# Attention with a mixture of experts: the squares kept in memory as turned, stored in 2 KB runs and read in 512-byte runs

## The chip, the cores and the metric

The kernel runs on one core of a Trainium2 chip. The metric is the device time of one execution in microseconds. Of the version before there are three runs: 2153.48, 2156.42 and 2159.98 us, median 2156.42 us.

## The reference, cut to what matters

There are 8 batches of 2496 tokens with 256 channels. Attention has no softmax: its weights are squares of clipped scores, and the scores are of z with itself, so that the matrix of weights is symmetric. Then each row goes through the one expert of eight that its gate picks.

```python
scores = scale * np.matmul(z, z.transpose(0, 2, 1))     # symmetric; z is 8 x 2496 x 64
attn = np.maximum(scores, 0.0) ** 2
out = np.matmul(attn, v)                                # v is 8 x 2496 x 256
x = (u * out).reshape(B * S, D)
...
e_idx = np.argmax(logits, axis=1)                       # logits = x @ w_gate + bias of the modality
h = np.maximum(x[mask] @ w1[e], 0.0)
out[mask] = gate_w[mask, None] * (h @ w2[e])
```

## The kernel before, in words

**Two parts.** The first part is the attention with the gate and the scattering of rows to their experts; it ends at about 1279 us. The second part runs the experts over tiles of 512 rows and is not touched by the change.

**Chunks and steps.** In the attention part each batch has five chunks of query columns, four of width 512 and a last one of 448. A chunk is worked through in ten steps, one for each pair of key tiles (2 x 128 keys). A step holds a tile r of 128 partitions (keys) x 2 x 512 (the two key tiles, the chunk's queries). For a step that is computed afresh, TensorE (PE) makes the scores (`scores`, line 334), ScalarE (ACT) clips and scales them (`root`, line 345) and squares them (`square`, line 394). Every step then has its squares split into a rounded part ah (`high`, line 418, on ACT or VectorE) and a rest al (`low`, line 427, on VectorE, called DVE), and PE multiplies both with the values v into the accumulators (`weigh`, line 451). `low` stands on DVE always, so PE waits for DVE in every step.

**Turned squares.** Since the matrix is symmetric, the block of keys q and queries c is the transpose of the block of keys c and queries q. For most pairs of chunks the kernel computes one of the two, transposes it on DVE in blocks of 32 x 32 (`turn_squares`, line 364, into one of two buffers named turn), stores it in memory (`store_squares`, lines 377 and 381) and reads it back when the other chunk needs it (`load_turned`, line 354), in place of scores, root and square. Of diagonal blocks one half is treated so (`is_half`: one half of the columns is computed, the other is read). In memory a block is a 512 x 512 matrix in the order in which the reader wants it. So the blocks of 32 x 32, which the transpose leaves in their places among the partitions, have to be put in order by the store: one transfer for each group of 32 partitions, with runs of 64 floats (256 bytes), in the last step of a chunk six transfers with runs of 32 floats. The load is then one transfer with runs of 4 KB for each partition.

**Who sets the order.** A planner in the kernel lists all pieces of work with an estimated cost and the step by which they are due, plays five queues (PE, ACT, DVE, GpSimd, SyncE's DMA queue) with these costs, and emits the instructions of each engine in the order in which the pieces came up. The order is then fixed; each engine works through its own in order and waits where an input or a buffer is missing. The costs are constants in the source: a transpose stands with 1.18 us (0.62 for a half), a store and a load with the numbers that the change edits. Pieces marked "AD" (`high`) go to whichever of ACT and DVE is free in that play. Buffers: six tiles r (tag a), four ah, four al, two turn.

```python
x = st_a[g].rearrange("p n (t i) -> p n t i", i=BLK)                      # turn_squares
nc.vector.transpose(out=y.rearrange(order, n=2)[:, :, t], in_=x[:, :, t])
...
src = squares[i // 2, c, b % 2].rearrange("(s p k) q -> s p k q", s=2, k=2)  # load_turned
nc.sync.dma_start(out=a[:, :, :w], in_=src[i % 2, :, :, :w])
```

Other lines that the text speaks of: 565 sums the gate's partial products (`take_gates`, a reduction over elements 32 bytes apart), 589 and 647 are small reductions of the routing (over neighbours, and over elements 80 bytes apart), 888 is the transpose of the second part, 547 and 557 turn the rows of a finished chunk, 507 and 511 evacuate its accumulators.

Of the kernel before, what the change touches and what calls it, by code (L numbers as in the profile page):

```python
# [9 lines left out]
F32 = mybir.dt.float32  # L10
# [6 lines left out]
P = 128  # L17
T = 512
# [9 lines left out]
def tile_attention_moe(ctx: ExitStack, tc: tile.TileContext, ut, v, zt, mid, wg, mb, w1, w2, out):  # L28
# [41 lines left out]
    xs = dram.tile([E * CAP, XW], F32, name="xs")  # L70
    places = dram.tile([MAXT, 2], I32, name="places")
    pairs |= {(c, c) for c in range(NCH - 1)}
    squares = {(q, c, e): dram.tile([T, T], F32, name=f"squares{q}_{c}_{e}") for q, c in pairs for e in range(2)}


    ident_r = const.tile([P, P], F32R, name="ident")
# [228 lines left out]
    def is_half(g):  # L305
        b, c, i = steps[g]
        return halved(b, c) and i == 2 * c + 1
# [8 lines left out]
    def is_turned(g):  # L316
        b, c, i = steps[g]
        return i // 2 < c and turns(b, i // 2, c)
# [18 lines left out]
    def root(g):  # L337
        w = columns(g)
        s = st_s.pop(g)
        if is_half(g):  # L340
            r = st_a[g]
        else:
            r = bulk.tile([P, 2, T], F32, tag="a", bufs=NA, name="r") if g else first_root
        for t in range(2) if g < 2 else (slice(0, 2),):
            nc.scalar.activation(out=r[:, t, w], in_=s[t][:, w] if g < 2 else s[:, :, w], func=AF.Relu, scale=INV)  # L345
        st_s[g] = r

    def load_turned(g):

        b, c, i = steps[g]  # L350
        w = H if is_half(g) else width[c]
        a = bulk.tile([P, 2, T], F32, tag="a", bufs=NA, name="r")
        src = squares[i // 2, c, b % 2].rearrange("(s p k) q -> s p k q", s=2, k=2)
        nc.sync.dma_start(out=a[:, :, :w], in_=src[i % 2, :, :, :w])
        st_a[g] = a

    def turn_squares(g):

        b, c, i = steps[g]
        y = raw.tile([P, T // BLK, 2 * BLK], F32, tag="turn", bufs=2, name="turn")  # L360
        order = "p t (i n) -> p n t i" if i < NI - 1 else "p t (n i) -> p n t i"
        t = slice(H // BLK if i == 2 * c else 0, T // BLK)
        x = st_a[g].rearrange("p n (t i) -> p n t i", i=BLK)
        nc.vector.transpose(out=y.rearrange(order, n=2)[:, :, t], in_=x[:, :, t])  # L364
        st_t[g] = y

    def store_squares(g):

        b, c, i = steps[g]
        y = st_t.pop(g)  # L370
        dst = squares[c, i // 2, b % 2].rearrange("(t i) k -> i t k", i=BLK)
        for n in range(P // BLK):
            mine = y[n * BLK:(n + 1) * BLK]
            if i < NI - 1:
                k0 = i % 2 * H + n * 2 * BLK
                t = slice(H // BLK if i == 2 * c else 0, T // BLK)
                nc.sync.dma_start(out=dst[:, t, k0:k0 + 2 * BLK], in_=mine[:, t])  # L377
            else:
                for k in range(2 if n < 2 else 1):
                    k0 = (J // 2 + k) * P + n * BLK  # L380
                    nc.sync.dma_start(out=dst[:, :, k0:k0 + BLK], in_=mine[:, :, k * BLK:(k + 1) * BLK])  # L381

    roots = {}

    def square(g):
        w = columns(g)
        a = r = st_s.pop(g)
        if g < 2:

            a = bulk.tile([P, 2, T], F32, tag="a", bufs=NA, name="r")  # L390
            roots[g] = r
        for t in (range(2),) if g else ((0,), (1,)):
            t = slice(t[0], t[-1] + 1)
            nc.scalar.square(out=a[:, t, w], in_=r[:, t, w])  # L394
        st_a[g] = a

    def first_high(g):
# [14 lines left out]
    def high(g):  # L412
        if g in roots:
            return first_high(g)
        w = width[steps[g][1]]
        ah = bulk.tile([P, 2, T], F32R, tag="ah", bufs=DEPTH, name="ah")
        copy = {"D": nc.vector.tensor_copy, "A": nc.scalar.copy}[by[g]]
        copy(out=ah[:, :, :w], in_=st_a[g][:, :, :w])  # L418
        st_h[g] = ah

    def low(g):
        _, c, i = steps[g]
        w = width[c]
        a, ah = st_a[g], st_h[g]
        al = bulk.tile([P, 2, T], F32R, tag="al", bufs=DEPTH, name="al")
        if i < NI - 1:
            nc.vector.tensor_tensor(out=al[:, :, :w], in0=a[:, :, :w], in1=ah[:, :, :w].bitcast(F32), op=ALU.subtract)  # L427
        else:
            nc.vector.tensor_tensor(out=al[:, 0, :w], in0=a[:, 0, :w], in1=ah[:, 0, :w].bitcast(F32), op=ALU.subtract)
            nc.vector.tensor_tensor(  # L430
                out=al[64:P, 1, :w], in0=a[64:P, 1, :w], in1=ah[64:P, 1, :w].bitcast(F32), op=ALU.subtract
            )
        st_h[g] = (ah, al)
# [551 lines left out]
    def step_pieces(n):  # L985
        b, c, i = steps[n]
        f = scale[c]
        high_after = None
        hold_a = Hold("a", 1 + is_source(n))
        read = None  # L990
        if is_turned(n) or is_half(n):
            src = [stored[b, i // 2, 2 * c + k] for k in range(1 if is_half(n) else 2)]
            read = transfer(0.7 if is_half(n) else 1.4, n - LEAD - (4 if is_half(n) else 2.5), load_turned, n, after=src, take=[hold_a], gate=n - LEAD - (6.0 if is_half(n) else 4))
            high_after = (read, 0.2)
        if not is_turned(n) and n >= MADE:
            f /= 1 + is_half(n)
            hold_s = Hold("s")
            p = piece(
                "P", 0.69 * f, n - LEAD, scores, n, after=[done_z.get((b, c)), done_z.get((b, i // 2)), scored.get("last")],
                take=[hold_s], drop=[hold_z[k] for k in {(b, c), (b, i // 2)}],  # L1000
            )
            scored["last"] = (p, 0.0)
            p = piece("A", 0.95 * f + 0.06, n - LEAD + 0.3, root, n, after=[(p, 0.25), (read, 0.2)], take=() if read else [hold_a], drop=[hold_s])
            p = piece("A", 0.95 * f + 0.06, n - LEAD + 1.0, square, n, after=[p])
            f = scale[c]
            high_after = (p, 0.08)
        if n > 0:
            own = n in (1,)
            p = piece(
                "D" if own else "AD", 1.3 if own else 0.93 * f, n - 1.8, high, n,  # L1010
                after=[high_after, (read, 0.2), split.get("high")], take=[Hold("ah")],
                drop=[Hold("a")] if n == 1 else (),
            )
            split["high"] = (p, 0.0)
            hold_h = [p.take[0], Hold("al")]
            if is_source(n):
                hold_t = Hold("turn")
                t = piece("D", 0.62 if i == 2 * c else 1.18, n - 1.5 if i == 2 * c else n + 0.5, turn_squares, n, after=[high_after], take=[hold_t], drop=[hold_a])
                stored[b, c, i] = transfer(1.4 if i == 2 * c else 2.8, n - 1.4 if i == 2 * c else n + 0.4, store_squares, n, issues=4 if i < NI - 1 else 6, after=[t])
                later.append((stored[b, c, i], hold_t))  # L1020
                begun.append(stored[b, c, i])
            p = piece(
                "D", 1.16 * f + 0.05, n - 1.1, low, n, after=[(p, 0.12), split.get("low")], take=hold_h[1:], drop=[hold_a],
            )
            split["low"] = (p, 0.0)
            ready = [(split["high"][0], 0.15), (p, 0.15 - 1.75 * f)]
        else:
            hold_h, ready = [Hold("ah"), Hold("al")], []
        v_of = hold_v[b, i // 2]
        ready += [done_v.get((b, i // 2)), weighed.get("last")]  # L1030
        first = i == first_step[b, c]
        if first:
            own = acc_hold[b, c] = [[Hold("bank") for _ in range(2)] for _ in range(KD)]
        us = (2.74 if i < NI - 1 else 2.05) * f
        if first and n:
            p = begun_chunk["half"] = piece("P", us / 2, n, weigh, n, 0, after=ready, take=own[0])
            p = piece("P", us / 2, n + 0.1, weigh, n, 1, after=[(p, 0.0)], take=own[1], drop=hold_h + v_of)
        elif n > 1 and i == second_step[b, c] and i < NI - 1:
            ready[-1] = (begun_chunk["half"], 0.0)
            h = piece("P", us / 2, n - 0.95, weigh, n, 0, after=ready)  # L1040
            p = piece("P", us / 2, n, weigh, n, 1, after=[(h, 0.0), weighed["last"]], drop=hold_h + v_of)
        else:
            p = piece("P", us, n, weigh if n else issued, n, after=ready, take=own[0] + own[1] if first else (), drop=hold_h + v_of)
        weighed["last"], weighed[n] = (p, 0.0), p
        p.step = n
# [508 lines left out]
```

## Time and profile before

| what | value |
|---|---|
| runs, median (lowest to highest) | 2156.42 us (2153.48 to 2159.98) |
| profiled execution, its own time | 2161.44 us |
| its span in the profile | 2159.0 us |
| PE, DVE, ACT busy in the span | 2128.9, 1650.3, 1422.8 us |
| mean granted clock of TensorE | 0.995 |
| bytes moved | 373.21 MB in 605497 packets |
| packets under 512 bytes | 522810 |
| transposes of squares | 189 (158 full, 31 half) |
| loads of turned squares | 189 |

How to read the rows. A row of a group names line, engine, operation, output and inputs, shape and count; then the busy time in us and the mean of one in ns; then the engine's idle time before these instructions and what ended it. A row of a stretch gives its bounds and length, and for each engine its busy time with the number of instructions; where it is asked for one line, those instructions alone are counted. A row of waits reads: who waited for whom, total us, times, longest. A row of the chain that ended last gives start, length and what it is. DMA share is the mean busy share of the 16 DMA engines.

### The profile page before, as it was taken

How to read it: one execution, taken by the hardware profiler on the slowest of the kernel's cores; microseconds unless marked ns; L12 is line 12 of the kernel's file. 1: busy time of each engine (PE TensorE's matmuls, PEld its weight loads, DVE VectorE, ACT ScalarE, POOL GpSimd, SP SyncE). 2: the span in 40 equal slices, each digit the busy share in tenths (PEclk: the TensorE clock that was granted, in tenths of full speed). 3: DMA queues.
4: the chain of work that ended last, by engine and by line, in shares of the span. 5: the costliest groups of instructions: out<-in, count | busy, mean ns of one | idle time of the engine just before them, and what ended most of it. 6: DMA issues, size and time to landing. Idle time of an engine off the chain costs nothing.

```text
span 2159.0 us, 44814 instructions
## 1 busy us (share of the span) xinstructions
PE 2128.9 (99%) x17190; PEld 1900.2 (88%) x17190; DVE 1650.3 (76%) x2292; ACT 1422.8 (66%) x2031; POOL 351.5 (16%) x342
## 2 busy tenths in 40 slices
PE   9999999999999999999999999999999999999997
PEld 7889999989989988888999988888888888888886
DVE  8889888878889889888888876666666666666664
ACT  8668868869768769779778753455455555454553
POOL 0000220210220210210310503112121211112121
PEclk9999999999999999999999999999999999999999
DMA  8976977977877978968968843645454544545451
GB/s 180 260 229 140 236 215 145 233 204 147 222 213 145 232 208 168 240 188 176 251 167 177 240 123 98 179 121 163 127 161 133 145 149 132 161 126 166 120 156 36
DMA packets 605497, 373.21 MB, mean 173 GB/s; under 512 B 522810, under 2 KB 547642, under 8 KB 605274
## 3 DMA queue, kind: packets, MB, share of 16 engines
q1 hardware_dynamic: 590186, 329.06, 60.8%
q0 software_dynamic: 15088, 41.21, 5.1%
q8 instruction: 136, 2.23, 0.4%
q14 instruction: 87, 0.71, 0.1%
HBM read 237.84 MB, written 132.31 MB: 171 GB/s over the span
## 4 chain that ended last, share of the span: by engine, by line
PE 86%; DMA 4%; issue 3%; DVE 3%; ACT 2%; SPq 1%; POOL 0%; POOLq 0%; DVEq 0%; ACTq 0%
PE acc L451 41%; PE ph L1268 18%; PE po L1279 12%; PE s L334 6%; PE po L1283 6%; DMA out_dram<-y,ids 2%; PE po L547 2%; DMA squares<-turn 1%; DMA r<-squares 1%; DVE al L427 1%; SPq L377 1%; ACT r L345 1%; ACT r L394 1%; DVE turn L364 0%; SPq L381 0%
## 5 line engine op out<-in xcount | busy, mean ns | idle before, releaser
L451 PE MATMUL acc<-ah,vh 64*128 64x512 f32 (+1 forms) x3120 | 468.6, 386 | 3.5 <-DVE ah L418 3.3
L451 PE MATMUL acc<-al,vh 64*128 64x512 f32 (+1 forms) x3120 | 456.5, 383 | 3.9 <-DVE al L427 3.9
L451 PE MATMUL acc<-ah,vl 64*128 64x512 f32 (+1 forms) x3120 | 455.9, 383 | 0.0
L427 DVE TENSOR_TENSOR al<-r,ah 128x1024 fp32r<-128x1024 f32 (+1 forms) x359 | 421.4, 1184 | 37.5 <-ACT ah L418 32.4
L1268 PE MATMUL ph<-xh,w 128*128 128x512 f32 x1248 | 399.5, 390 | 0.1
L1273 DVE SCALAR_TENSOR_TENSOR hl<-ph,hh 128x512 fp32r<-128x512 f32 x312 | 211.4, 688 | 236.3 <-ACT hh L1272 209.9
L1272 ACT ACTIVATE hh<-ph 128x512 fp32r<-128x512 f32 x312 | 187.1, 600 | 303.3 <-PE ph L1268 236.1
L671 POOL DMA_INDIRECT xs<-x,sloti x160 | 193.8, 1211 | 1076.4 <-ACT ah L418 492.6
L451 PEld LDWEIGHTS acc<-al,vh 64*128 64x128 f32 x3120 | 342.0, 185 | 28.6 <-DVE al L427 5.1
L451 PEld LDWEIGHTS acc<-ah,vh 64*128 64x128 f32 x3120 | 337.2, 185 | 28.7 <-DVE ah L418 3.7
L451 PEld LDWEIGHTS acc<-ah,vl 64*128 64x128 f32 x3120 | 337.3, 185 | 23.6
L418 ACT CAST ah<-r 128x1024 fp32r<-128x1024 f32 (+1 forms) x281 | 285.7, 1033 | 78.9 <-PE acc L451 46.6
L1279 PE MATMUL po<-w,hh 128*128 128x512 f32 x1248 | 296.7, 389 | 0.0
L345 ACT ACTIVATE r<-s 128x1024 f32<-128x1024 f32 (+2 forms) x244 | 235.7, 967 | 83.8 <-PE s L334 72.4
L1268 PEld LDWEIGHTS ph<-xh,w 128*128 128x128 f32 x1248 | 234.6, 188 | 47.8 <-issue 0.6
L1279 PEld LDWEIGHTS po<-w,hh 128*128 128x128 f32 x1248 | 234.1, 188 | 48.3
L1292 POOL DMA_INDIRECT out_dram<-y,ids x157 | 152.7, 973 | 721.2 <-DVE y L1320 686.2
L364 DVE STREAM_TRANSPOSE turn<-r 128x1024 f32<-128x1024 f32 (+1 forms) x189 | 217.0, 1151 | 41.1 <-DMA squares<-turn 27.6
L394 ACT ACTIVATE r<-r 128x1024 f32<-128x1024 f32 (+2 forms) x243 | 242.8, 999 | 5.7
L1268 PE MATMUL ph<-xl,w 128*128 128x512 f32 x624 | 243.7, 391 | 0.1
L334 PE MATMUL s<-zm 64*128 64x512 f32 (+2 forms) x1452 | 211.9, 383 | 5.2 <-ACT r L345 4.9
L869 DVE TENSOR_TENSOR w<-wq,w 128x1024 fp32r<-128x1024 f32 x148 | 177.8, 1221 | 19.3 <-ACT w L865 19.0
(158 smaller groups left out, 2013.1 us busy)
## 6 DMA issues: line engine op xcount, KB each, us to landing
wq<-in_moe_w_dram SPq DMA_DIRECT2D x148, 512.0 KB
squares<-turn SPq DMA_DIRECT2D x508, 128.0 KB
r<-squares SPq DMA_DIRECT2D x96, 512.0 KB
r<-squares SPq DMA_DIRECT2D x62, 448.0 KB
ut<-in_ut_dram SPq DMA_DIRECT2D x40, 512.0 KB
xg<-xs SPq DMA_DIRECT2D x156, 128.0 KB
squares<-turn SPq DMA_DIRECT2D x310, 64.0 KB
vr<-in_v_dram SPq DMA_DIRECT2D x32, 512.0 KB
```

What stands on the lines that cost most here:

```text
L334: nc.tensor.matmul(out=s[t][:, w], lhsT=lhs, rhs=mv[halves[t], ql, w], start=n == 0, stop=n == 2)
L345: nc.scalar.activation(out=r[:, t, w], in_=s[t][:, w] if g < 2 else s[:, :, w], func=AF.Relu, scale=INV)
L364: nc.vector.transpose(out=y.rearrange(order, n=2)[:, :, t], in_=x[:, :, t])
L394: nc.scalar.square(out=a[:, t, w], in_=r[:, t, w])
L418: copy(out=ah[:, :, :w], in_=st_a[g][:, :, :w])
L427: nc.vector.tensor_tensor(out=al[:, :, :w], in0=a[:, :, :w], in1=ah[:, :, :w].bitcast(F32), op=ALU.subtract)
L451: nc.tensor.matmul(out=acc[b, c][r][dh][:, :w], lhsT=V[b, k // J][y][halves[r], k % J, dh * P:(dh + 1) * P], rhs=x[halves[r], k % 2, :w], ...
L671: nc.gpsimd.indirect_dma_start(out=xs, out_offset=bass.IndirectOffsetOnAxis(ap=RT[b]["sloti"][:n, k:k + 1], axis=0), in_=x[:n, j, :], in_o ...
L1268: nc.tensor.matmul(out=ph, lhsT=lhs, rhs=rhs[:, k, :], start=n == 0, stop=n == 3 * KD - 1)
L1272: nc.scalar.activation(out=hh, in_=ph, func=AF.Relu)
L1273: nc.vector.scalar_tensor_tensor(out=hl, in0=ph, scalar=0.0, in1=hh.bitcast(F32), op0=ALU.max, op1=ALU.subtract)
L1279: nc.tensor.matmul(out=po[j], lhsT=x, rhs=both, start=f == 0, stop=False, skip_group_check=True)
```

## The change

Squares now lie in memory as the transpose leaves them, by partition and not by key. The tile in memory is [half of the chunk's columns, key tile of the pair, 128 partitions, 512]. The store is one transfer for each block, 2 KB runs on the memory side. The load puts the groups of 32 partitions in order: for each partition eight runs of 128 floats (512 bytes). For that the columns that go into one 32 x 32 block are no longer 32 neighbours but every eighth of 256 columns, so that 8 such blocks of a half lie behind each other in a stored row.

What a load brings is then, within a partition, in groups of 64 columns that alternate between the two key tiles (`blocks`); `high` and `low` read it in that order through `views` and write their parts ah and al in the old order. In the last chunk, whose width is 448, a turned step has three different pieces of columns, and `high` and `low` take three instructions each. A half step's computed columns are written into the same grouped order by `root`, and its square runs over 512 neighbouring elements. In the planner the costs of a load (0.7 and 1.4 become 1.1 and 2.2) and of a store (1.4 and 2.8 become 0.9 and 1.7) are edited and the store has one issue; the cost of a transpose is not.

```diff
-    squares = {(q, c, e): dram.tile([T, T], F32, name=f"squares{q}_{c}_{e}") for q, c in pairs for e in range(2)}
+    squares = {(q, c, e): dram.tile([2, 2, P, T], F32, name=f"squares{q}_{c}_{e}") for q, c in pairs for e in range(2)}
...
     def load_turned(g):
...
-        w = H if is_half(g) else width[c]
         a = bulk.tile([P, 2, T], F32, tag="a", bufs=NA, name="r")
-        src = squares[i // 2, c, b % 2].rearrange("(s p k) q -> s p k q", s=2, k=2)
-        nc.sync.dma_start(out=a[:, :, :w], in_=src[i % 2, :, :, :w])
+        src = squares[i // 2, c, b % 2][i % 2, 0:1 if is_half(g) else 2].rearrange("s (n i) (m x) -> (i m) (s n) x", i=BLK, m=4)
+        x = a.rearrange("p k (g x) -> p (k g) x", x=P)
+        nc.sync.dma_start(out=x[:, 0:src.shape[1]], in_=src)
...
+    def blocks(a):
+        return a.rearrange("p k t -> p (k t)").rearrange("p (g k w) -> p k g w", k=2, w=64)
...
+    def views(g, a, *split):
...
+        y = blocks(a)
+        if c < NCH - 1:
+            return [[y] + [in_blocks(x) for x in split]]
+        at = [slice(0, H), slice(H, H + P), slice(H + P, w)]
+        parts = [y[:, :, 0:4], y[:, :, 4:8, 0:BLK], y[:, :, 4:6, BLK:]]
...
     def turn_squares(g):
...
-        x = st_a[g].rearrange("p n (t i) -> p n t i", i=BLK)
-        nc.vector.transpose(out=y.rearrange(order, n=2)[:, :, t], in_=x[:, :, t])
+        x = st_a[g].rearrange("p n (h i t) -> p n h t i", h=2, i=BLK)
+        y4 = y.rearrange(order, n=2, i=BLK)
+        if i == 2 * c:
+            nc.vector.transpose(out=y4[:, :, 1], in_=x[:, :, 1])
+        else:
+            nc.vector.transpose(out=y4, in_=x)
...
     def store_squares(g):
...
-        for n in range(P // BLK):
-            mine = y[n * BLK:(n + 1) * BLK]
...
-                nc.sync.dma_start(out=dst[:, t, k0:k0 + 2 * BLK], in_=mine[:, t])
...
+        dst = squares[c, i // 2, b % 2][h, i % 2].rearrange("h p f -> p h f")
+        nc.sync.dma_start(out=dst, in_=y[:, h])
...
     def high(g):
...
-        copy(out=ah[:, :, :w], in_=st_a[g][:, :, :w])
+        for x, y in views(g, st_a[g], ah):
+            copy(out=y, in_=x)
...
     def low(g):
...
-            nc.vector.tensor_tensor(out=al[:, :, :w], in0=a[:, :, :w], in1=ah[:, :, :w].bitcast(F32), op=ALU.subtract)
+            for x, h, y in views(g, a, ah, al):
+                nc.vector.tensor_tensor(out=y, in0=x, in1=h.bitcast(F32), op=ALU.subtract)
...
-                stored[b, c, i] = transfer(1.4 if i == 2 * c else 2.8, n - 1.4 if i == 2 * c else n + 0.4, store_squares, n, issues=4 if i < NI - 1 else 6, after=[t])
+                stored[b, c, i] = transfer(0.9 if i == 2 * c else 1.7, n - 1.4 if i == 2 * c else n + 0.4, store_squares, n, after=[t])
```

More of the change, by code (lines that the diff above doesn't have):

```diff
@@ L341, in root @@
             r = st_a[g]
-        else:
-            r = bulk.tile([P, 2, T], F32, tag="a", bufs=NA, name="r") if g else first_root
+            nc.scalar.activation(out=blocks(r)[:, :, H // 64:], in_=in_blocks(s[:, :, w]), func=AF.Relu, scale=INV)
+            st_s[g] = r
+            return
+        r = bulk.tile([P, 2, T], F32, tag="a", bufs=NA, name="r") if g else first_root
         for t in range(2) if g < 2 else (slice(0, 2),):
@@ L350, in load_turned, with in_blocks @@
         b, c, i = steps[g]
-        w = H if is_half(g) else width[c]
         a = bulk.tile([P, 2, T], F32, tag="a", bufs=NA, name="r")
-        src = squares[i // 2, c, b % 2].rearrange("(s p k) q -> s p k q", s=2, k=2)
-        nc.sync.dma_start(out=a[:, :, :w], in_=src[i % 2, :, :, :w])
+        src = squares[i // 2, c, b % 2][i % 2, 0:1 if is_half(g) else 2].rearrange("s (n i) (m x) -> (i m) (s n) x", i=BLK, m=4)
+        x = a.rearrange("p k (g x) -> p (k g) x", x=P)
+        nc.sync.dma_start(out=x[:, 0:src.shape[1]], in_=src)
         st_a[g] = a
+    def blocks(a):
+        return a.rearrange("p k t -> p (k t)").rearrange("p (g k w) -> p k g w", k=2, w=64)
+    def in_blocks(x):
+        return x.rearrange("p k (g w) -> p k g w", w=64)
+    def views(g, a, *split):
+        _, c, i = steps[g]
+        w = width[c]
+        if not is_turned(g) and not is_half(g):
+            return [[x[:, :, :w] for x in (a, *split)]]
+        y = blocks(a)
[3 more added lines that the diff above has]
+        parts = [y[:, :, 0:4], y[:, :, 4:8, 0:BLK], y[:, :, 4:6, BLK:]]
+        return [[v] + [x[:, :, t].rearrange("p k (g w) -> p k g w", g=v.shape[2]) for x in split] for v, t in zip(parts, at)]
     def turn_squares(g):
         b, c, i = steps[g]
-        y = raw.tile([P, T // BLK, 2 * BLK], F32, tag="turn", bufs=2, name="turn")
-        order = "p t (i n) -> p n t i" if i < NI - 1 else "p t (n i) -> p n t i"
-        t = slice(H // BLK if i == 2 * c else 0, T // BLK)
-        x = st_a[g].rearrange("p n (t i) -> p n t i", i=BLK)
-        nc.vector.transpose(out=y.rearrange(order, n=2)[:, :, t], in_=x[:, :, t])
+        y = raw.tile([P, 2, T], F32, tag="turn", bufs=2, name="turn")
+        order = "p h (t i n) -> p n h t i" if i < NI - 1 else "p h (t n i) -> p n h t i"
+        h = slice(1 if i == 2 * c else 0, 2)
+        x = st_a[g].rearrange("p n (h i t) -> p n h t i", h=2, i=BLK)
[4 more added lines that the diff above has]
+            nc.vector.transpose(out=y4, in_=x)
         st_t[g] = y
@@ L370, in store_squares @@
         y = st_t.pop(g)
-        dst = squares[c, i // 2, b % 2].rearrange("(t i) k -> i t k", i=BLK)
-        for n in range(P // BLK):
-            mine = y[n * BLK:(n + 1) * BLK]
[L374 to L381, printed above, removed]
+        h = slice(1 if i == 2 * c else 0, 2)
+        dst = squares[c, i // 2, b % 2][h, i % 2].rearrange("h p f -> p h f")
+        nc.sync.dma_start(out=dst, in_=y[:, h])
     roots = {}
@@ L391, in square @@
             roots[g] = r
-        for t in (range(2),) if g else ((0,), (1,)):
-            t = slice(t[0], t[-1] + 1)
-            nc.scalar.square(out=a[:, t, w], in_=r[:, t, w])
+        if is_half(g):
+            nc.scalar.square(out=a[:, 1, :], in_=r[:, 1, :])
+        else:
+            for t in (range(2),) if g else ((0,), (1,)):
+                t = slice(t[0], t[-1] + 1)
+                nc.scalar.square(out=a[:, t, w], in_=r[:, t, w])
         st_a[g] = a
@@ L414, in high @@
             return first_high(g)
-        w = width[steps[g][1]]
         ah = bulk.tile([P, 2, T], F32R, tag="ah", bufs=DEPTH, name="ah")
         copy = {"D": nc.vector.tensor_copy, "A": nc.scalar.copy}[by[g]]
-        copy(out=ah[:, :, :w], in_=st_a[g][:, :, :w])
+        for x, y in views(g, st_a[g], ah):
+            copy(out=y, in_=x)
         st_h[g] = ah
@@ L992, in step_pieces @@
             src = [stored[b, i // 2, 2 * c + k] for k in range(1 if is_half(n) else 2)]
-            read = transfer(0.7 if is_half(n) else 1.4, n - LEAD - (4 if is_half(n) else 2.5), load_turned, n, after=src, take=[hold_a], gate=n - LEAD - (6.0 if is_half(n) else 4))
+            read = transfer(1.1 if is_half(n) else 2.2, n - LEAD - (4 if is_half(n) else 2.5), load_turned, n, after=src, take=[hold_a], gate=n - LEAD - (6.0 if is_half(n) else 4))
             high_after = (read, 0.2)
```

## The prediction

> **What bounds the kernel now.** I read the page first: one execution of 2159.0 us, its engines, its DMA queues and the shares of the chain that ended last.
>
> ```profile
> span 2159.0 us, 44814 instructions
> PE 2128.9 (99%) x17190; PEld 1900.2 (88%) x17190; DVE 1650.3 (76%) x2292; ACT 1422.8 (66%) x2031; POOL 351.5 (16%) x342
> ...
> q1 hardware_dynamic: 590186, 329.06, 60.8%
> q0 software_dynamic: 15088, 41.21, 5.1%
> ...
> PE 86%; DMA 4%; issue 3%; DVE 3%; ACT 2%; SPq 1%; POOL 0%; POOLq 0%; DVEq 0%; ACTq 0%
> ```
>
> TensorE carries 86% of the chain, DMA 4%. All squares are moved before 1279 us, in the attention part, so I cut that part out of the span (columns: length; busy time of PE, PEld, DVE, ACT, POOL with their counts; granted clock; DMA share; GB/s), and beside it the transposes of line 364 alone.
>
> ```profile
> 18.00:1279.00 1261.00, 1245.30 (x12642) 1147.51 (x12638) 1082.11 (x1451) 976.79 (x1341) 184.13 (x155) 0.99 0.80 199
> ```
> ```profile
> 18.00:1279.00 1261.00, 217.04 (x189) 0.99 0.80 199
> ```
>
> PE idles 1261.0 - 1245.3 = 15.7 us there. That is all that a faster DMA can give back directly. VectorE (DVE) is idle for 178.9 us, ACT for 284.2 us. The average hides how DVE's work lies, so next come the five chunks of one whole batch (the fourth), from one evacuation of the accumulators to the next; then line 364 alone in the same five, and a chunk of the next batch.
>
> ```profile
> 494.10:526.80 32.70, 32.70 (x319) 29.95 (x318) 28.98 (x34) 29.02 (x39) 0.00 (x0) 1.00 0.89 176
> 526.80:560.10 33.30, 33.18 (x351) 30.80 (x345) 29.58 (x48) 29.01 (x43) 0.00 (x0) 1.00 0.76 156
> 560.10:592.20 32.10, 32.10 (x326) 31.38 (x324) 27.67 (x38) 24.03 (x33) 13.55 (x11) 1.00 0.92 257
> 592.20:625.70 33.50, 30.69 (x297) 25.18 (x296) 24.49 (x33) 17.83 (x27) 11.59 (x10) 0.95 0.99 271
> 625.70:654.80 29.10, 29.10 (x322) 26.39 (x322) 25.99 (x30) 23.81 (x35) 0.62 (x2) 1.00 0.37 105
> sum 160.70, PE 157.76 PEld 143.69 DVE 136.72 ACT 123.71 POOL 25.76; mean PE 31.55 PEld 28.74 DVE 27.34 ACT 24.74 POOL 5.15
> ```
> ```profile
> 494.10:526.80 32.70, 9.39 (x8) 1.00 0.89 176
> 526.80:560.10 33.30, 7.31 (x6) 1.00 0.76 156
> 560.10:592.20 32.10, 5.66 (x5) 1.00 0.92 257
> 592.20:625.70 33.50, 3.18 (x3) 0.95 0.99 271
> 625.70:654.80 29.10, 1.94 (x2) 1.00 0.37 105
> ```
> ```profile
> 687.50:720.20 32.70, 32.70 (x347) 31.87 (x342) 31.81 (x52) 27.43 (x41) 0.94 (x1) 1.00 0.76 162
> ```
>
> DVE is close behind PE. It is busy 28.98 of 32.7 us in a batch's first chunk, which has 8 of the batch's 24 transposes, and in the chunk of the last row 31.81 of 32.70 us, 97%, with PE never idle. So 97% can be had; I take it as what DVE can reach.
>
> **The DMA side.** These are the waits on squares, two links of the chain before two of PE's gaps, and the issues on SP.
>
> ```profile
> DVE turn L364 <- DMA squares<-turn: 27.6, 21, 3.6
> ...
> ACT ah L418 <- DMA r<-squares: 21.9, 13, 4.7
> ```
> ```profile
> 127.60 7.35 DMA r<-squares
> ```
> ```profile
> 587.27 7.77 DMA squares<-turn
> ```
> ```profile
> squares<-turn SPq DMA_DIRECT2D x508, 128.0 KB
> r<-squares SPq DMA_DIRECT2D x96, 512.0 KB
> ...
> squares<-turn SPq DMA_DIRECT2D x310, 64.0 KB
> ```
> ```profile
> L377 SPq DMA_DIRECT2D squares<-turn x632: 302/515/3237, 19.3 to 1228.7; - x158
> ```
>
> A full store is 2048 runs of 256 bytes now and 256 runs of 2 KB after; a full load is 128 runs of 4 KB now and 1024 of 512 bytes after. The two queue lines give a price: time of 16 engines = packets x a + bytes x b. For q1 that is 0.608 x 2159 x 16 = 21,000 us, for q0 0.051 x 2159 x 16 = 1,760 us; solved, a is 15 ns and b 0.037 ns per byte. On each of 16 engines a store falls from 128 x 24 ns = 3.1 us to 16 x 91 ns = 1.5 us, and a load grows from 8 x 168 ns = 1.3 us to 64 x 34 ns = 2.2 us. Over all stores some 387,000 packets become 44,000, over all loads some 36,000 become 178,000: 200,000 fewer at 15 ns on 16 engines are about 190 us, and the DMA share of the attention part falls from 0.80 to about 0.65. On SP four to six issues of 0.5 us become one: 508 + 310 = 818 issues become 189, and a load no longer stands behind such a run of them.
>
> The order on SP, batch 0, its first chunk (squares0_1_0 is the buffer of chunks 0 and 1), before and then after:
>
> ```order
> L377 DMA squares0_1_0_62<-turn_347 32x16x64 x4
> L377 DMA squares0_1_0_62<-turn_427 32x16x64 x4
> L377 DMA squares0_2_0_82<-turn_470 32x16x64 x4
> L354 DMA r_516<-squares0_1_0_62 128x1024
> L377 DMA squares0_2_0_82<-turn_523 32x16x64 x4
> ```
> ```order
> L399 DMA squares0_1_0_62<-turn_347 128x2x512
> L399 DMA squares0_1_0_62<-turn_424 128x2x512
> L399 DMA squares0_2_0_82<-turn_464 128x2x512
> L356 DMA r_479<-squares0_1_0_62 128x8x128
> L399 DMA squares0_2_0_82<-turn_514 128x2x512
> ```
>
> The places stay, four issues shrink to one, and the load becomes eight pieces per partition. I expect most of the 27.6 us of DVE's wait for a free turn buffer to go, and some 10 of PE's 15.7 us. A load that is 0.9 us longer stays covered, because the issue order puts it several steps ahead; if it were not, ACT's 21.9 us of waiting would grow.
>
> **The DVE side.** Here are the groups by shape that price a strided read and a cut instruction.
>
> ```profile
> L427 DVE TENSOR_TENSOR al<-r,ah 128x896 fp32r<-128x896 f32 x72 | 76.8, 1086 | 4.7 <-ACT ah L418 3.0 <-PE acc L451 0.6
> L364 DVE STREAM_TRANSPOSE turn<-r 128x1024 f32<-128x1024 f32 x158 | 195.4, 1239 | 27.7 <-DMA squares<-turn 17.0 <-ACT r L394 6.1 <-issue 4.0
> L364 DVE STREAM_TRANSPOSE turn<-r 128x512 f32<-128x512 f32 x31 | 21.8, 704 | 13.4 <-DMA squares<-turn 10.6 <-ACT r L345 1.5 <-issue 1.4
> L888 DVE STREAM_TRANSPOSE xt<-xg 128x1024 f32<-128x1024 f32 x39 | 48.2, 1235 | 0.0
> L565 DVE TENSOR_REDUCE lg<-rb 128x32 f32<-128x384 f32 x40 | 36.2, 904 | 12.9 <-ACT rb L558 12.1 <-ACT x L557 0.8
> L647 DVE TENSOR_REDUCE slot<-run 128x20 f32<-128x160 f32 x9 | 4.0, 441 | 0.3
> L589 DVE TENSOR_REDUCE mx<-lg 128x20 f32<-128x160 f32 x7 | 2.2, 320 | 0.2
> L589 DVE TENSOR_REDUCE mx<-lg 128x8 f32<-128x64 f32 x1 | 0.2, 220 | 0.0
> ```
>
> *The transpose.* It used to read 32 neighbouring columns per block; after the change it reads every eighth column, a step of 32 bytes from element to element. No transpose of before reads so. Two reductions do: line 565 steps 32 bytes, line 647 steps 80. Line 589 reads neighbours: (320 - 220)/96 = 1.04 ns an element and 153 ns fixed. At that rate the 384 elements of line 565 would take 553 ns; they take 904, so 0.91 ns more for each. Line 647 takes 121 ns more for 160, 0.76 each. A full transpose of 1024 elements then grows from 1239 ns to 2175 ns (by line 565) or 2015 ns (by line 647), a half one by half as much. I take line 565, whose step is the same. Over the part: 158 x 0.936 + 31 x 0.468 = 162 us more of DVE (134 us by line 647; nothing, if the transposing array does not feel the step). A step of 8 bytes costs nothing: line 364 writes so today and takes 1239 ns, line 888 writes neighbours and takes 1235.
>
> [...]
>
> *The cut instructions.* The 62 turned steps in the short last chunks (width 448) now take three instructions for each split, because their columns are three blocks. This is DVE in batch 0 where chunk 4 begins (ah is the rounded part, al the rest, x the evacuated chunk 3), before and after:
>
> ```order
> L418 CAST ah<-r 128x2x448
> L427 TENSOR_TENSOR al<-r,ah 128x2x448
> L511 TENSOR_TENSOR x<-acc,x 128x4x128 x2
> L518 TENSOR_TENSOR x<-x,ut 128x4x256
> L427 TENSOR_TENSOR al<-r,ah 128x2x448
> L536 TENSOR_TENSOR x<-x,rb 128x4x256
> ```
> ```order
> L439 CAST ah<-r 128x2x256
> L439 CAST ah<-r 128x2x128
> L439 CAST ah<-r 128x2x64
> L449 TENSOR_TENSOR al<-r,ah 128x2x256
> L449 TENSOR_TENSOR al<-r,ah 128x2x128
> L449 TENSOR_TENSOR al<-r,ah 128x2x64
> L533 TENSOR_TENSOR x<-acc,x 128x4x128 x2
> L540 TENSOR_TENSOR x<-x,ut 128x4x256
> ```
>
> Each split of a turned step has become three rows. The elements are the same; the fixed part, 1086 - 896 x 1.04 = 154 ns, is paid twice more. 62 on al and 23 on DVE's ah: 85 x 2 x 0.154 = 26 us on DVE, 3.4 us in each last chunk. The other 39 ah lie on ACT, some 12 us within 284 us of idle time: nothing. Reading blocks of 64 neighbouring columns (256 bytes) in the other turned steps I cost at nothing.
>
> **The sum.** DVE's work in the attention part becomes 1082 + 162 + 26 = 1270 us, in a part that is 1261 us long. By chunks of the batch shown (full and half transposes from line 364's times): 28.98 + 7.0, 29.58 + 5.6, 27.67 + 4.2, 24.49 + 2.3, and 25.99 + 1.4 + 3.4, so 36.0, 35.2, 31.9, 26.8 and 30.8 us against lengths of 32.7, 33.3, 32.1, 33.5 and 29.1. At 97% busy the chunks need 37.1, 36.3, 32.9, 27.6 and 31.8 us. If no chunk can lend to another, four of them grow by 4.4 + 3.0 + 0.8 + 2.7 = 10.9 us: 87 us over eight batches, 77 less PE's 10 us of gaps. If they lend freely, the batch needs 160.7/0.97 = 165.7 us instead of 160.7: 40 us. DVE's order is fixed and only four al buffers let it run ahead, so I take the middle, 58 us, and round down to 54 because line 647 speaks for a lower price. The profiled execution took 2161.4 us with what lies around its span, the median of the runs is 5 us less: 2156.4 + 54 = 2210 us. By line 647 and free lending DVE needs 1242/0.97 = 1280 us, 19 us more: 2176. By line 565 without lending or closed gaps: 2243.
>
> **The rivals.** *The transpose does not feel the step.* [...] Then DVE gains only the 26 us, the last chunks stand at 29.4 of 29.1 us, which costs 2 to 9 us over the batches, and PE's gaps close by 10 to 15: 2143 to 2156, likeliest 2149, faster. It decides at about 1.65 us a transpose, where DVE's first two chunks reach 97%. [...] Chance 0.14, more than half of it faster.
>
> *The step costs more, or the loads are late.* [...] If each of 189 loads were waited for by its extra 0.9 us, up to 170 us would come; the lead of several steps and a lighter queue speak against it. Chance 0.07.
>
> *The step is felt, but buffers absorb it*: under 6 us, against a DVE total above the part's length. Chance 0.03.
>
> **The numbers.** Main case 0.76, from 2176 to 2243. A measurement of this kernel tells 0.3% (6.5 us) from no change. Faster 0.08, all from the free transpose; same 0.11, the rest of that rival, the absorbing one and the main case's low edge; slower 0.81. The range runs from 2152, so that it takes in part of the free transpose, to 2255, a little above the main case without lending.
>
> **What would show it.** Line 390's transposes at 2.0 to 2.2 us; DVE above 95% in the first two chunks of a batch and PE's idle time there put down to al or ah; stores and DVE's wait for turn buffers shorter; a DMA share near 0.65; 1279 us moved to about 1333, and the part behind it unchanged. A full transpose under 1.4 us makes the forecast wrong.

## The result and the profile after

The changed kernel takes 2210.67 us (median of 6 runs, 2209.19 to 2213.85) beside 2156.28 us before; the ratio is 1.0255, 95% interval [1.0241, 1.0268]. It is slower by 2.5%, at the time that was forecast (2210 us). (In two of the experiments below one run each, of 4392 and of 3019 us, was in a slow state, and the medians leave it out.) First the page after, the attention part, and the five chunks of the fourth batch (columns as before: bounds, length, busy PE, PEld, DVE, ACT, POOL with counts, clock, DMA share, GB/s).

```profile
span 2207.3 us, 44115 instructions
PE 2141.8 (97%) x17190; PEld 1853.0 (84%) x17190; DVE 1809.7 (82%) x2460; ACT 1432.3 (65%) x2111; POOL 392.4 (18%) x342
...
q1 hardware_dynamic: 379034, 337.15, 50.6%
```
```profile
18.00:1326.40 1308.40, 1258.10 (x12632) 1100.07 (x12628) 1240.37 (x1618) 984.66 (x1420) 224.90 (x155) 0.99 0.63 197
```
```profile
502.40:539.30 36.90, 34.58 (x338) 29.10 (x336) 36.73 (x36) 28.11 (x39) 0.00 (x0) 1.00 0.47 153
539.30:576.70 37.40, 32.80 (x321) 28.14 (x323) 36.42 (x51) 28.15 (x42) 0.33 (x1) 1.00 0.48 153
576.70:609.40 32.70, 31.92 (x320) 26.37 (x318) 32.51 (x38) 23.30 (x31) 15.31 (x11) 1.00 0.93 303
609.40:638.90 29.50, 29.50 (x302) 24.17 (x300) 24.53 (x38) 19.18 (x32) 11.76 (x8) 1.00 0.88 265
638.90:667.10 28.20, 28.20 (x316) 25.62 (x314) 27.43 (x48) 23.21 (x40) 3.85 (x2) 1.00 0.41 119
```

The attention part ends at 1326.4 us in place of 1279.0: 47.4 us. Of these PE is idle for 34.6 (50.3 us of the part in place of 15.7); its busy time, for the same matmuls, grew by 12.8. The two profiled executions, of 2161.44 and 2209.19 us, lie only 48 us apart, mainly because the one of before was 5 us above its median. What lies behind the attention part is unchanged, 2207.3 - 1326.4 = 880.9 us against 880.0. In the first two chunks DVE is busy for 36.73 of 36.90 and 36.42 of 37.40 us, and PE, which was never idle there for more than 0.2 us, now is for 2.3 and 4.6 us. The fourth chunk became shorter, 29.5 in place of 33.5 us: there PE used to wait for squares and was idle for 2.8 us. In that this batch is not typical. These are the mean lengths of the five chunks over the second to the eighth batch, each from the start of one evacuation on ACT to the next:

| kernel | first | second | third | fourth | last | batch |
|---|---|---|---|---|---|---|
| before | 33.3 | 33.0 | 32.0 | 31.2 | 28.5 | 157.9 us |
| after | 35.5 | 38.5 | 32.7 | 29.9 | 28.1 | 164.8 us |

So most of the growth of 6.9 us a batch lies in the second chunk. The groups say why DVE is full.

```profile
L390 DVE STREAM_TRANSPOSE turn<-r 128x1024 f32<-128x1024 f32 x158 | 345.7, 2188 | 10.5 <-ACT r L415 9.5 <-issue 0.8
L388 DVE STREAM_TRANSPOSE turn<-r 128x512 f32<-128x512 f32 x31 | 36.0, 1161 | 1.8 <-DMA squares<-turn 1.8
```
```profile
L449 DVE TENSOR_TENSOR al<-r,ah 128x1024 fp32r<-128x1024 f32 (+4 forms) x483 | 428.8, 921 | 6.0 <-ACT ah L439 4.0
```

A full transpose went from 1239 to 2188 ns, a half one from 704 to 1161. Now who waits for squares, and what PE waits for.

```profile
  ACT ah L439: 2.1, 1
  DVE turn L388: 1.8, 1
```
```profile
PE pc L657 <- DVE cnt L648: 16.8, 7, 3.6
PE s L334 <- ACT r L347: 9.8, 10, 2.3
PE acc L473 <- DVE al L449: 8.6, 10, 1.7
PE po L569 <- DVE rb L554: 6.6, 6, 1.9
```

The waits for squares are almost gone (21.9 and 27.6 us before). PE's new waits are for pieces that DVE reaches late, and for r from ACT. The largest is not for al, but for the routing's count (`cnt`), which stands in the second chunk of a batch; PE waits for it seven times.

### The profile page after: what moved, and what is told of

Same layout as the page of the kernel before. It is cut to its first block, busy times and chain, and to the rows that moved or that the text cites. A ratio compares the mean times of both kernels' runs of the same rounds, so it can differ in the third digit from the quotient of the medians.

```text
span 2207.3 us, 44115 instructions
## 1 busy us (share of the span) xinstructions
PE 2141.8 (97%) x17190; PEld 1853.0 (84%) x17190; DVE 1809.7 (82%) x2460; ACT 1432.3 (65%) x2111; POOL 392.4 (18%) x342
## 4 chain that ended last, share of the span: by engine, by line
PE 43%; DVE 6%; issue 3%; DMA 2%; ACT 0%; POOL 0%; POOLq 0%; DVEq 0%; ACTq 0%
PE ph L1290 18%; PE po L1301 12%; PE acc L473 7%; PE po L1305 6%; DVE turn L390 2%; DMA out_dram<-y,ids 2%; DVE al L449 2%; PE s L334 1%; PE po L569 0%; DVE ah L439 0%; DVE x L558 0%; DVE x L540 0%; DVE x L533 0%; DVE lg L587 0%; POOL out_dram L1314 0%
## 5 line engine op out<-in xcount | busy, mean ns | idle before, releaser
L473 PE MATMUL acc<-ah,vl 64*128 64x512 f32 (+1 forms) x3120 | 449.5, 384 | 0.0
L449 DVE TENSOR_TENSOR al<-r,ah 128x1024 fp32r<-128x1024 f32 (+4 forms) x483 | 428.8, 921 | 6.0 <-ACT ah L439 4.0
L693 POOL DMA_INDIRECT xs<-x,sloti x160 | 234.9, 1468 | 1080.0 <-ACT ah L439 375.4
L473 PEld LDWEIGHTS acc<-al,vh 64*128 64x128 f32 x3120 | 324.6, 185 | 56.1 <-DVE al L449 15.9
L473 PEld LDWEIGHTS acc<-ah,vh 64*128 64x128 f32 x3120 | 321.3, 185 | 41.9 <-ACT ah L439 2.3
L390 DVE STREAM_TRANSPOSE turn<-r 128x1024 f32<-128x1024 f32 x158 | 345.7, 2188 | 10.5 <-ACT r L415 9.5
L473 PEld LDWEIGHTS acc<-ah,vl 64*128 64x128 f32 x3120 | 320.7, 185 | 37.6 <-DVE vl L261 0.4
L439 ACT CAST ah<-r 128x1024 fp32r<-128x1024 f32 (+4 forms) x361 | 295.6, 852 | 54.8 <-PE acc L473 41.4
L347 ACT ACTIVATE r<-s 128x1024 f32<-128x1024 f32 (+2 forms) x213 | 216.6, 1018 | 91.8 <-PE s L334 77.7
L415 ACT ACTIVATE r<-r 128x1024 f32<-128x1024 f32 (+2 forms) x212 | 222.9, 1052 | 5.0
```

What stands on the lines that cost most here:

```text
L390: nc.vector.transpose(out=y4, in_=x)
L439: copy(out=y, in_=x)
L449: nc.vector.tensor_tensor(out=y, in0=x, in1=h.bitcast(F32), op=ALU.subtract)
L473: nc.tensor.matmul(out=acc[b, c][r][dh][:, :w], lhsT=V[b, k // J][y][halves[r], k % J, dh * P:(dh + 1) * P], rhs=x[halves[r], k % 2, :w], ...
L693: nc.gpsimd.indirect_dma_start(out=xs, out_offset=bass.IndirectOffsetOnAxis(ap=RT[b]["sloti"][:n, k:k + 1], axis=0), in_=x[:n, j, :], in_o ...
```

## The experiments

Theory: a transpose that steps 32 bytes from element to element makes DVE the bound of the first chunks. Rivals: the new loads or the new order of the pieces, the cut instructions, and, for what it is worth to take work off DVE, the place of the long transposes in the order.

**The step alone, taken out of after.**

```diff
-        x = st_a[g].rearrange("p n (h i t) -> p n h t i", h=2, i=BLK)
+        x = st_a[g].rearrange("p n (h t i) -> p n h t i", h=2, i=BLK)
```

> The kernel after, but each transpose block reads 32 neighbouring columns again (the blocks then hold the wrong columns; stores, loads, order and planner are those of after). Theory (the 32-byte step makes DVE the bound): transposes back to 1.24 us, DVE at most 95% busy in any chunk, PE's gaps before squares gone as in after, time 2143 to 2152 us, a little under before. Rival (the new loads or the new order of the pieces cost the time): still 2195 us or more. Rival (the cut instructions of the last chunks): still 2185 us or more.

Measured: 2138.31 us, ratio to before 0.9922 [0.9905, 0.9939]. Its attention part, and its transposes:

```profile
18.00:1257.20 1239.20, 1235.70 (x12634) 1178.57 (x12630) 1087.24 (x1618) 985.55 (x1420) 184.19 (x155) 1.00 0.67 208
```
```profile
L390 DVE STREAM_TRANSPOSE turn<-r 128x1024 f32<-128x1024 f32 x158 | 195.6, 1238 | 26.7 <-ACT r L415 25.2 <-DMA squares<-turn 1.3
```

PE is idle for 3.5 us of 1239.2. So the step costs 72 us, and everything else in the change together (long runs, fewer issues, the planner's new order) gains 18 us, more than the 4 to 13 that were expected. As causes of the slowdown both rivals, loads and cut instructions, fall. The mean chunks are 33.1, 33.5, 31.6, 29.6 and 28.1 us here, 155.8 a batch: the step alone adds 2.4, 5.0, 1.1, 0.3 and 0.0 us to them, some 8.9 a batch. The first chunk has most of the transposes, but the second pays most.

**The step alone, put into before.**

```diff
-        x = st_a[g].rearrange("p n (t i) -> p n t i", i=BLK)
...
+        x = st_a[g].rearrange("p n (h i t) -> p n h t i", h=2, i=BLK)
```

> The kernel before with one edit: the transpose reads every eighth column (the blocks then hold the wrong columns); stores, loads, order and planner are those of before. Theory: full transposes at 2.19 us, DVE's work in the attention part 1082 + 162 us, no cut instructions but the old waits for squares: 2205 to 2225 us, as slow as after or slower. Rival (loads, order): 2153 to 2160 us, as before.

Measured: 2231.26 us, ratio 1.0350 [1.0331, 1.0370]; 75 us more than before.

```profile
L368 DVE STREAM_TRANSPOSE turn<-r 128x1024 f32<-128x1024 f32 x158 | 345.0, 2187 | 13.9 <-ACT r L398 7.0 <-DMA squares<-turn 6.5 <-issue 0.2
```

The price is the same 2187 ns, and the kernel is 21 us slower than after: my range stopped 6 us short, since it left too little for the gain of the rest. The two experiments agree: 72 and 75 us for the step, 18 and 21 us for the rest.

**The cut instructions.**

```diff
+        return [[y[:, :, 0:7]] + [in_blocks(x[:, :, :w]) for x in split]]
```

> The kernel after, but in the last chunks one instruction in place of three splits a turned step (the columns are then in the wrong places). Theory: the last chunks are already at PE's pace in after (28.1 of 28.1 us), so the 26 us of DVE work that go are worth 0 to 5 us: 2205 to 2211 us. Rival (the cut instructions carry a good part, as the sum of the prediction had it with 2.7 us a batch): 2185 to 2195 us.

Measured: 2209.73 us against 2210.67: nothing, as the theory had it. The prediction's 2.7 us a batch for the last chunks were wrong, and so was its work: without the cuts DVE is busy for 1231.31 us of the part in place of 1240.37, so they cost it 9 us and not 26.

**What a step costs by its length.** In one run the transposes differ in the reading order. The block of a chunk's last step (its last pair of key tiles) takes every second column. The other full blocks take, by their chunk of queries from the first to the fourth, 16 pairs of neighbours 32 columns apart, every fourth column, every eighth and every sixteenth.

```diff
+        if i == NI - 1:
+            nc.vector.transpose(out=y3.rearrange("p n (g t) i -> p n g t i", t=2), in_=st_a[g].rearrange("p n (g i t) -> p n g t i", t=2, i=BLK))
...
+            if c == 0:
+                nc.vector.transpose(out=yp, in_=st_a[g].rearrange("p n (i t u) -> p t n i u", t=16, u=2))
+            elif c == 1:
+                nc.vector.transpose(out=y3.rearrange("p n (g t) i -> p n g t i", t=4), in_=st_a[g].rearrange("p n (g i t) -> p n g t i", t=4, i=BLK))
+            elif c == 2:
+                nc.vector.transpose(out=y4, in_=x)
+            else:
+                nc.vector.transpose(out=y3, in_=st_a[g].rearrange("p n (i t) -> p n t i", t=16, i=BLK))
```

> The kernel after with other reading orders in its transposes (the blocks hold the wrong columns), one per chunk of queries, to price the step alone: chunk 0 reads pairs of neighbours 32 columns apart, chunk 1 every fourth column (16 bytes), chunk 2 every eighth (32), chunk 3 every sixteenth (64), the last key tiles every second (8). [...] Rival (every step that is not to the neighbour costs, by its length): 8 bytes 1.5 us or more, pairs in between, 64 bytes more than 32.

Lines 390, 395, 397, 399 and 401 are the five, in the order of the diff:

```profile
L397 DVE STREAM_TRANSPOSE turn<-r 128x1024 f32<-128x1024 f32 x40 | 81.0, 2026 | 0.0
L395 DVE STREAM_TRANSPOSE turn<-r 128x1024 f32<-128x1024 f32 x56 | 69.3, 1240 | 4.4 <-ACT r L432 4.1 <-DMA squares<-turn 0.3
L399 DVE STREAM_TRANSPOSE turn<-r 128x1024 f32<-128x1024 f32 x24 | 52.6, 2191 | 3.7 <-ACT r L432 3.7
...
L390 DVE STREAM_TRANSPOSE turn<-r 128x1024 f32<-128x1024 f32 x31 | 38.4, 1240 | 3.0 <-ACT r L432 3.0
...
L401 DVE STREAM_TRANSPOSE turn<-r 128x1024 f32<-128x1024 f32 x7 | 13.9, 1993 | 4.2 <-ACT r L432 4.2
```

8 bytes and pairs take 1240 ns, no more than neighbours (1239 in before); 16 bytes take 2026 ns, 32 bytes 2191, 64 bytes 1993. So the rival falls, by which every step costs by its length: it had 8 bytes at 1.5 us or more, and 64 bytes above 32. What makes the price jump between 8 and 16 bytes is not shown; a step of 12 bytes was not run. The whole took 2168.3 us in one run.

**Work off DVE, on to ACT.** First by the planner's own cost:

```diff
-                t = piece("D", 0.62 if i == 2 * c else 1.18, n - 1.5 if i == 2 * c else n + 0.5, turn_squares, n, after=[high_after], take=[hold_t], drop=[hold_a])
+                t = piece("D", 1.16 if i == 2 * c else 2.19, n - 1.5 if i == 2 * c else n + 0.5, turn_squares, n, after=[high_after], take=[hold_t], drop=[hold_a])
```

> The kernel after, all of it computed; only the planner's cost of a transpose is 2.19 us (half: 1.16) in place of 1.18 (0.62). It moves 49 of 115 roundings into ah from DVE to ACT, some 36 us of DVE work. Theory (DVE's work in the first chunks sets the time): 20 to 36 us less than after, 2175 to 2191 us, still slower than before, since 1270 - 36 us of DVE work against 1261 us leave the first two chunks over-full. Rival (loads or DMA set the time): 2205 to 2215 us.

Measured: 2204.32 us, ratio 1.0233 [1.0214, 1.0253]: 5 to 6 us less than after, with intervals that still overlap, and not 20 to 36. The attention part, and a wait that is back:

```profile
18.00:1321.50 1303.50, 1254.73 (x12628) 1081.44 (x12626) 1214.65 (x1551) 1028.58 (x1485) 220.75 (x155) 0.99 0.63 198
```
```profile
ACT ah L439 <- DMA r<-squares: 22.3, 13, 4.3
```

DVE lost 25.7 us of work, ACT got 43.9, and loads are waited for again. So I moved the roundings with the order kept:

```diff
-                by[p.args[0]] = e
+                by[p.args[0]] = "A" if steps[p.args[0]][1] < 3 and p.args[0] > 1 else e
```

> The kernel after, all of it computed, with the order of all pieces as in after; only the 59 roundings into ah that stand on DVE in the first three chunks of the batches are done by ACT, at the same place of the order: some 41 us less DVE work where DVE is over-full, 62 us more on ACT, which idles 280 us. Theory (DVE's work in these chunks sets the time, and the planner with the true cost failed only because its new order moved work and loads): 25 to 38 us less than after, 2172 to 2186 us. Rival (order and loads, not DVE's work, set the time): 2203 us or more, as with the true cost.

Measured: 2206.33 us, ratio 1.0243 [1.0222, 1.0265]. Again a miss: 3 to 4 us less than after, with intervals that overlap, in place of 25 to 38:

```profile
18.00:1324.90 1306.90, 1259.51 (x12632) 1119.07 (x12630) 1211.15 (x1561) 1038.40 (x1478) 215.93 (x155) 0.99 0.63 198
```

DVE's busy time fell by 29.2 us, ACT's grew by 53.7. My theory in the form "DVE's sum sets the time" predicted too much. Two further runs ask whether ACT ate the relief. The first makes the same move where transposes are cheap:

```diff
-        x = st_a[g].rearrange("p n (h i t) -> p n h t i", h=2, i=BLK)
+        x = st_a[g].rearrange("p n (h t i) -> p n h t i", h=2, i=BLK)
...
-                by[p.args[0]] = e
+                by[p.args[0]] = "A" if steps[p.args[0]][1] < 3 and p.args[0] > 1 else e
```

> The kernel whose transposes read 32 neighbours (wrong columns in the blocks), with the 59 roundings of the first three chunks on ACT in place of DVE. Theory A (ACT, at 90% in the first chunk, falls behind its order by itself): 2145 us or more, against 2138 without the move. Theory B (ACT bears it, only the transposes matter): 2136 to 2141 us.

Measured: 2149.74 us, ratio 0.9974 [0.9963, 0.9985]: the move alone costs 11.4 us, with DVE relieved by 30.8 us and ACT burdened by 50.8 (1036.35 against 985.55):

```profile
18.00:1267.70 1249.70, 1238.93 (x12630) 1171.37 (x12626) 1056.41 (x1560) 1036.35 (x1479) 185.02 (x155) 1.00 0.66 207
```

ACT's idle time, 254 us of this part without the move, is no cover. DVE waits longer for what ACT now rounds; the first row is without the move, the second with it:

```profile
DVE al L449 <- ACT ah L439: 28.6, 41, 2.5
```
```profile
DVE al L449 <- ACT ah L439: 51.5, 62, 4.5
```

The second takes work off DVE and gives it to nobody:

```diff
-        x = oT[b, c][:, :, 0:D]
-        nc.vector.tensor_tensor(out=x, in0=x, in1=U.pop((b, c)), op=ALU.mult)
+        d = 8 if c in (0, 1, NCH - 1) else D
+        x = oT[b, c][:, :, 0:d]
+        nc.vector.tensor_tensor(out=x, in0=x, in1=U.pop((b, c))[:, :, 0:d], op=ALU.mult)
...
-        nc.vector.tensor_tensor(out=x, in0=x, in1=parted[b, c][0], op=ALU.subtract)
+        nc.vector.tensor_tensor(out=x, in0=x, in1=parted[b, c][0][:, :, 0:d], op=ALU.subtract)
```

> The kernel after, order unchanged; two VectorE operations on the rows of a finished chunk (times u, and minus the rounded part) work on 32 of 1024 elements where they fall into the first three chunks of a batch: 1.22 us become some 0.2 us, about 47 us less DVE work there, and nothing goes to ACT (most of the multiplication by u is left out). It asks why 41 us less DVE work with the roundings on ACT gave 4 us. Theory A (DVE's work in these chunks sets the time, and the earlier relief was eaten by ACT, which fell behind in turn): 30 to 45 us less than after, 2166 to 2181 us. Theory B (not DVE's sum but the place of each long transpose in the fixed order sets the time, ahead of a piece that PE waits for): 0 to 15 us less, 2196 to 2211 us.

Measured: 2180.81 us (three runs), ratio 1.0126 [1.0093, 1.0159]: 28 to 30 us less than after, at the edge of theory A's range.

```profile
18.00:1296.50 1278.50, 1248.77 (x12630) 1105.65 (x12626) 1196.03 (x1618) 984.48 (x1419) 214.15 (x155) 1.00 0.65 202
```

Busy DVE fell by 44.3 us and the part by 29.9: DVE's work does set the time, at about two thirds of its price. In the kernel with mixed steps 83.7 us less (1156.66 busy) brought 39.6, in the one with neighbours 153.1 us less brought 69.2, about half. On that scale the 29 us that the move took off DVE are worth an estimated 13 to 20 us. If the 11 us that the move costs where transposes are cheap come off in full, which was not tested, 2 to 9 are left; 3 to 4 were measured.

**PE's longest wait.** The count of the routing, placed later by the planner:

```diff
-        p = piece("P", 0.3, need + 1.4, route_count, b, cols, after=[(p, 0.15)], take=hold)
+        p = piece("P", 0.3, need + 1.4, route_count, b, cols, after=[(p, 5.0)], take=hold)
```

> The kernel after, all of it computed; the planner places the four matmuls that count the routing (PE waits 16.8 us for their input from DVE in after, once a batch in the second chunk) some 5 us later than their input's end. Theory A (DVE's sum sets the time): PE's wait moves to the next al, 0 to 6 us less than after, 2204 to 2211 us. Theory B (the single places where PE meets a late piece set it): some 15 us less, 2192 to 2198 us.

Measured: 2219.01 us, ratio 1.0293 [1.0268, 1.0317], 8 us more than after, which neither theory had. The wait for the count is gone, others stand in its place:

```profile
PE acc L473 <- DVE al L449: 12.5, 14, 2.4
PE po L569 <- DVE rb L554: 11.6, 9, 2.2
PE acc L473 <- DVE base L665: 6.3, 4, 2.4
```

The planner wrote another order all over the part, with 11.5 us more work on DVE; taking out PE's largest wait in this way gained nothing, and what that wait costs by itself this run can't say.

**The DMA side.** Loads in long runs, and stores in four, both with neighbours in the transpose:

```diff
-        src = squares[i // 2, c, b % 2][i % 2, 0:1 if is_half(g) else 2].rearrange("s (n i) (m x) -> (i m) (s n) x", i=BLK, m=4)
+        src = squares[i // 2, c, b % 2][i % 2]
+        if is_half(g):
+            src = src[0].rearrange("p (g x) -> p g x", x=P)
+        else:
+            src = src.rearrange("s (q e) (g x) -> (s q) (e g) x", e=2, x=P)
```

> The kernel with neighbours read by the transpose, and with loads in runs of 4 KB (2 KB for half steps) in place of 512 bytes (the wrong elements in the wrong places). Theory: loads wait in front, so their length is worth nothing, 2135 to 2140 us, as with 512 bytes. Rival (the longer loads cost time that the stores' gain hid): 2130 us or less.

Measured: 2136.95 us against 2138.31: loads of 128 packets in place of 1024 are worth 1.4 us by the medians and nothing by the ratios to before (0.9921 and 0.9922).

```diff
-        nc.sync.dma_start(out=dst, in_=y[:, h])
+        for k in range(P // BLK):
+            part = slice(k * BLK, (k + 1) * BLK)
+            nc.sync.dma_start(out=dst[part], in_=y[part, h])
```

> The kernel whose transposes read 32 neighbours (wrong columns in the blocks), with each store cut into four transfers of 32 partitions, runs still of 2 KB: SP issues 756 stores in place of 189. Theory (the shorter packets of the store are what freed the turn buffers and the loads): 2137 to 2142 us. Rival (the issues on SP are what the change saved): 2146 us or more.

Measured: 2140.50 us, 2 us more, though DVE waits longer for its turn buffers again:

```profile
DVE turn L390 <- DMA squares<-turn: 13.1, 12, 3.0
```

So of the 18 us only 2 or so come with the fewer issues. The rest comes with the long runs of the stores or with the new order that the planner made from the edited costs; no run separates these two.

**A version that beats both.** Transposes that read pairs of neighbours took 1240 ns, no more than with single neighbours, so blocks can be made of 16 pairs. A reader's run is then 64 floats. The planner's costs of a load and a store are edited with it.

```diff
+        order = "p (t i u n) -> p t n i u" if i < NI - 1 else "p (t n i u) -> p t n i u"
...
+            x = st_a[g].rearrange("p n (i t u) -> p t n i u", i=BLK // 2, u=2)
+            nc.vector.transpose(out=y.rearrange(order, n=2, i=BLK // 2, u=2), in_=x)
...
+        for u in range(2):
+            dst = squares[c, i // 2, b % 2][u]
+            nc.sync.dma_start(out=dst if i == 2 * c else dst[i % 2], in_=y[u::2, 0:w])
...
+            src = src.rearrange("u s (n h i) (t x) -> h (i t) (u s n) x", n=4, h=2, x=64)[i % 2]
+            nc.sync.dma_start(out=a.rearrange("p u (g x) -> p (u g) x", x=64), in_=src)
```

> All of it computed: blocks of 16 pairs of neighbouring columns are turned, stored in two transfers (even and odd partitions) of 4 KB runs and read in one transfer of 256-byte runs. Theory: pairs cost the transpose nothing (1.24 us), DVE stays below 97% in every chunk, stores stay short, loads are longer by an estimated 0.9 us than in after but wait in front: 2137 to 2150 us, below before. Rival (the shorter runs or the DMA load take it back): 2153 us or more. Rival (pairs cost as single columns do): 2200 us or more.

Measured: 2140.98 us (6 runs, 2140.52 to 2141.09), ratio to before 0.9939 [0.9927, 0.9952]: 0.6% faster than before, 3.2% than after.

```profile
18.00:1259.50 1241.50, 1236.80 (x12632) 1178.53 (x12630) 1085.89 (x1639) 992.17 (x1429) 178.58 (x155) 1.00 0.75 208
```
```profile
L376 DVE STREAM_TRANSPOSE turn<-r 128x1024 f32<-128x1024 f32 x158 | 195.8, 1240 | 25.2 <-ACT r L409 23.8 <-DMA squares<-turn 1.2
```

Transposes take 1240 ns; PE is idle for 4.7 us of the part in place of 15.7 before, although loads come in runs of 256 bytes.

## Why the prediction was right, point by point

- *The price of the step* (2175 ns from line 565, or 2015 from line 647): 2188 measured, 1161 for a half against 1172. Taking the row with the same step was right; line 647's step of 80 bytes stands near the 64-byte transpose (1993). This term decided the direction and most of the size.
- *What a gain is left by DMA* ("some 10 of PE's 15.7 us"): 18 us by the kernel with neighbours. It was mis-sized: the prediction took PE's idle time of 15.7 us for all that there was to gain, but PE's busy time itself fell too, from 1245.3 to 1235.7 us, beside its idle time, which fell to 3.5. Why the same matmuls were busy for less was not tested; the granted clock of the part is 0.99 in the one row and 1.00 in the other. The DMA share fell from 0.80 to 0.63 (0.65 was forecast) and loads stayed covered, as forecast.
- *The cut instructions* (26 us of DVE work, 2.7 us a batch in the last chunks): wrong. The al group grew by 7.4 us (421.4 to 428.8), not by 19, since short instructions in a row overlap in their records: 483 of 921 ns would be 445 us. The mean last chunk did not grow at all (28.5 to 28.1 us). That DVE does this work ahead, in the slack of the chunk in front, would fit, but is not shown.
- *The sum* (DVE at 97% at most; chunks that lend nothing, +10.9 us a batch, or freely, +5.0; the middle taken): neither picture held. Without the last chunk's 2.7 us the sum without lending is 4.4 + 3.0 + 0.8 = 8.2 us a batch, close to the 8.9 that the step alone costs. But chunks do pass work on: the first grew by 2.4 and the second by 5.0. For the batch shown 37.1, 36.3, 32.9, 27.6 and 31.8 us were worked out as what DVE needs, and 36.9, 37.4, 32.7, 29.5 and 28.2 came. DVE reached 99% in the first chunk, so 97% was too low a ceiling there, but over the whole part it reached 95% (1240.37 of 1308.40), and its work in the part is 1240 us, not 1270.
- So that the total came out within 1 us is in part luck. The step costs 72 to 75 us by the experiments, where the two sums gave 40 and 87 (some 20 of the 87 in the last chunks, where nothing came) and something between was taken; the rest gains 18 to 21 us, where the sum had 10. The step was put too low and the gain too low by about as much, and the two cancel. What was right is the mechanism: dearer transposes (2188 ns in place of 1239) fill DVE in a batch's first two chunks (36.73 of 36.90 and 36.42 of 37.40 us in the batch shown), and PE waits there (2.3 and 4.6 us).
- *Where PE would wait* (al or ah): only in part. The count of the routing, r and rb together cost PE more than al and ah do (33.2 us in the rows shown, beside 8.6 for al). That the move of roundings to ACT gave 3 to 4 us where 25 to 38 were expected shows that "DVE's work divided by 97%" is no price for a single repair. Shown is that the move costs too (11 us where transposes are cheap, for 51 us more on ACT) and that DVE's work alone returns a half to two thirds. Why not all of it, and which links of the order pass it on, stays open: a run that moves one piece to another place, with the order of the rest kept, was not made.
- *The rivals.* The free transpose fell with 2188 ns: at a step of 8 bytes the price is that of neighbours (1240 ns), at 16, 32 and 64 bytes it is not (2026, 2191 and 1993). The dearer step fell with (2188 - 1239)/1024 = 0.93 ns more an element, where the sum had 0.91, the late loads with 2.1 us of waiting for loads, and buffers that absorb the step with the 72 us that it costs.

## What to carry to other kernels

Before an access pattern is changed to please the DMA, look for an instruction in the trace that already reads by the new step, and take its excess per element: here one reduction of 40 calls gave the transpose's new price within 1%. A reading order that costs the transpose nothing (here pairs and 8 bytes, 1240 ns) may serve the DMA nearly as well: pairs kept most of the gain, 0.6% below before where neighbours stand 0.8% below it. Work moved from a full engine to one that is busy for three quarters of the time (ACT here) need not be relief: moving 29 us of DVE's work brought 3 to 4 us, taking 44 us away brought 28 to 30. And look at every batch before one is taken for all: the one shown here was not typical.

## What was not expected of the hardware

The cost of a step does not grow with its length: 16 bytes 2026 ns, 32 bytes 2191, 64 bytes 1993 for 1024 elements, against 1240 at 8 bytes and 1239 for neighbours. Which of 16, 32 and 64 bytes is dearest rests on that one run, with 40, 24 and 7 transposes. And DVE's records overlap: in before all its groups by line add up to 1744 us, beside 1650.3 us of busy time. Between before and after transposes, al and ah grow by 164.7, 7.4 and 1.2 us by their groups, 173 in all, its busy time by 159.4 us (1650.3 to 1809.7).
